# The second product of an MLP by Strassen's scheme, inside a fused attention and MLP kernel

## The chip, the cores and the metric

The kernel runs on one core of one Trainium2 chip. Times are device microseconds of that core. The engines are named as in the profile: PE does matrix products (PEld is its loading of weights), DVE is the vector engine, ACT the scalar engine with its function tables, POOL the general engine (here it masks, and issues the loads that convert f32 to f16), SP only issues DMAs. Every engine works off its own queue in order. Products are written to PSUM, eight banks of 512 f32 numbers per partition.

## The reference

Attention with a forgetting gate, for 8 batches, 8 heads, 576 tokens, head dimension 64, and then an MLP over all 4608 tokens:

```python
scores = q @ k.T / sqrt(64) + cum[i] - cum[j]      # cum: running sum of log f, causal mask
attn   = softmax(scores)
x      = (attn @ v)                                 # tokens x 512, heads side by side
h      = x @ w_in                                   # 512 -> 2048
g      = h - tanh(h)
out    = g @ w_out                                  # 2048 -> 512, f32
```

## The kernel before

**Attention pairs.** The heads of a batch are taken two at a time: 32 pairs p, pair p being heads 2c and 2c+1 of batch b, with p = 4b + c. For each pair `scores` (L256) makes seven tiles ti = 0 to 6 of transposed scores in PSUM; ACT takes the exponential (L262), POOL masks the diagonal blocks (L270). One pair later, between tiles 2 and 3, `values` (L280) multiplies by v, with a column of ones for the sums, and DVE divides (L284 to L286) into the tile xn.

**From attention to the MLP.** `turn` transposes xn into XR, a ring of 4 batches that holds x with the feature on the partition: for batch 0 by PE, from then on by two DMA transposes on SP's queue (L300: tokens 0 to 511 of the batch, L302: the last 64). It is emitted after tile 3 of the pair behind, so a batch's last pair (c = 3) is turned in the first pair of the next batch.

**The MLP** goes by units of 512 tokens, nine in all. A unit was a list of 32 steps: 16 `mlp1` steps, one for each block of 128 of the 2048 inner columns, and 16 `mlp2` steps. An `mlp1` step is four products of 128 x 128 x 512 (one for each c, in order) into one PSUM bank, tanh on ACT (L315), and an addition on DVE (L318) that leaves g for these 128 columns as an f16 tile gt. An `mlp2` step is four products of 128 x 128 x 512 (L326); four steps accumulate 128 tokens over all 16 blocks into one bank, ACT copies it to SBUF (L330), and SP stores it (L332).

**How they are mixed.** The MLP's steps are dealt out over the pairs. From pair 4 on, each pair takes the next `take` steps of the list of all units, and they are placed evenly between the pair's items (scores, values, transposes, turn), at the end of an item. The order on PE, POOL, SP and DVE is just the order of emission; each of these engines waits in that order. What is left of the list follows the last pair. `take` was 2 in pair 4, 8 in pair 5, 7 in pairs 6 to 9, then 8.

**Transposes of q and k.** For batches 0 to 2 PE transposes q and k (`trans`, L225) through PSUM, and DVE or ACT copies them out (L234); this goes on until pair 10. For later batches they are loaded by blocks (L86), turned by DMA into TQ and TK (L91, on SP's queue in the first two pairs of the batch before) and placed by DVE (L94).

**PSUM.** Two banks for scores, two for values, three (`ps_m`) that the MLP's tiles share in turn with the transposes of pairs 0 to 4, and one (`ps_tr`) for the later transposes. A buffer is given again when what reads it is done; for `mlp1` that is the addition on DVE.

**Loads.** w_in and w_out come in pieces of 1 MB (w_out is issued in pair 4); k, q and v of a batch come some pairs ahead, in pieces of 64 to 128 KB, issued by POOL after given tiles.

Of the kernel before, what the change touches and what calls it, by code (L numbers as in the profile page):

```python
# [8 lines left out]
FP32 = mybir.dt.float32  # L9
FP16 = mybir.dt.float16  # L10
AF = mybir.ActivationFunctionType
# [10 lines left out]
def kernel(  # L22
# [11 lines left out]
    P = 128  # L34
# [9 lines left out]
    qscale = float(D) ** -0.5  # L44
    inv_qscale = float(D) ** 0.5
    NFT = DFF // P
    NCH = DM // P
    UW = 512
    NU = NT // UW
# [3 lines left out]
    wpl = ctx.enter_context(tc.tile_pool(name="wpl", bufs=1))  # L53
    aex = ctx.enter_context(tc.tile_pool(name="aex", bufs=10))
    fin = ctx.enter_context(tc.tile_pool(name="fin", bufs=3))
    gtp = ctx.enter_context(tc.tile_pool(name="gtp", bufs=NFT + 6))
    tmp = ctx.enter_context(tc.tile_pool(name="tmp", bufs=2))
    PSUM = bass.MemoryType.PSUM
    ps_sc = ctx.enter_context(tc.tile_pool(name="ps_sc", bufs=2, space=PSUM))
    ps_av = ctx.enter_context(tc.tile_pool(name="ps_av", bufs=1, space=PSUM))  # L60
    ps_tr = ctx.enter_context(tc.tile_pool(name="ps_tr", bufs=1, space=PSUM))
    ps_m = ctx.enter_context(tc.tile_pool(name="ps_m", bufs=3, space=PSUM))

    win = wpl.tile([P, NCH, DFF], FP16)
    wout = wpl.tile([P, NFT, DM], FP16)
    RING = 4 * S
    XR = wpl.tile([P, NCH, RING], FP16)

# [39 lines left out]
    lf = cst.tile([NH, S], FP32)  # L108
# [9 lines left out]
    ones16 = cst.tile([NH, S], FP16)  # L118
    nc.vector.memset(ones16, 1.0)
    minus16 = cst.tile([2 * H, S], FP16)  # L120
# [13 lines left out]
    cum = cst.tile([NH, S], FP32)  # L134
    nc.vector.tensor_tensor_scan(out=cum, data0=ones16, data1=lf, initial=0.0,
                                 op0=ALU.mult, op1=ALU.add)
    chi = cst.tile([NH, S], FP16)
# [53 lines left out]
             (4, 2): [lambda: load_wout(NFT // 2, NFT)]}  # L191
    for n in range(NJ - 1):
        LOADS.setdefault((3, n), []).append(lambda n=n: load_v_block(1, n, 2, H))
    LOADS.setdefault((NPAIR, 5), []).append(lambda: load_qk(qn, q, 2, 0, H))
    LOADS.setdefault((NPAIR, 6), []).append(lambda: load_qk(kn, k, 2, 0, H))
    for b in range(2, B):
# [17 lines left out]
    E, XN, GT, M2 = {}, {}, {}, {}  # L214

    def trans(b, c, src, dst, early, copies):
        pn, g3 = S // NT6, NT6 // 2
        if early:
            t32 = ps_m.tile([P, UW], FP32, tag="m", name="t32")
            t16 = t32.bitcast(FP16)[:, 0:2 * S // 2].rearrange("p (a g n) -> p a g n", a=2, g=g3)  # L220
        else:
            t16 = ps_tr.tile([P, 2, g3, pn], FP16, tag="tr", name="t16")
        for a in range(2):
            for g in range(g3):
                nc.tensor.transpose(out=t16[:, a, g, :],  # L225
                                    in_=src[b % 2][:, 2 * c + a, 2 * g:2 * g + 2, :],
                                    identity=id16[0:pn, 0:pn])
        for e, eng in enumerate(copies):
            to = dst[b % 2][0:D, 2 * c:2 * c + 2, e:S:2].rearrange("d a (p g) -> d a p g", g=g3)
            of = t16[e * D:(e + 1) * D, :, :, :].rearrange("d a g p -> d a p g")  # L230
            if eng == "A":
                nc.scalar.activation(out=to, in_=of, func=AF.Copy)
            else:
                nc.vector.tensor_copy(out=to, in_=of)  # L234
# [66 lines left out]
                                    in_=xn[:, 0:NJ - 1, :].rearrange("p n d -> p (n d)"))  # L301
        nc.sync.dma_start_transpose(out=XR[:, c, r0 + S - D:r0 + S], in_=xn[D:P, NJ - 1, :])  # L302

    def mlp1(u, ft):
        hps = ps_m.tile([P, UW], FP32, tag="m", name="hps")
        t0 = u * UW % RING
        parts = [(0, t0, min(UW, RING - t0))]
        if t0 + UW > RING:
            parts.append((RING - t0, 0, t0 + UW - RING))
        for o, t, n in parts:  # L310
            for ci in range(NCH):
                nc.tensor.matmul(out=hps[:, o:o + n], lhsT=win[:, ci, ft * P:(ft + 1) * P],  # L312
                                 rhs=XR[:, ci, t:t + n], start=(ci == 0), stop=(ci == NCH - 1))
        th = tmp.tile([P, UW], FP32, tag="th", name="th")
        nc.scalar.activation(out=th, in_=hps, func=AF.Tanh, scale=-1.0)  # L315
        gt = gtp.tile([P, UW], FP16, tag="gt", name="gt")
        GT[(u, ft)] = gt
        nc.vector.tensor_tensor(out=gt, in0=hps, in1=th, op=ALU.add)  # L318

    def mlp2(u, s):  # L320
        m, part = divmod(s, 4)
        if part == 0:
            M2[u] = ps_m.tile([P, DM], FP32, tag="m", name="ops")
        ops = M2[u]
        for ft in range(part * 4, part * 4 + 4):
            nc.tensor.matmul(out=ops, lhsT=GT[(u, ft)][:, m * P:(m + 1) * P], rhs=wout[:, ft, :],  # L326
                             start=(ft == 0), stop=(ft == NFT - 1))
        if part == 3:
            ost = tmp.tile([P, DM], FP32, tag="ost", name="ost")
            nc.scalar.activation(out=ost, in_=ops, func=AF.Copy)  # L330
            r0 = u * UW + m * P
            nc.sync.dma_start(out=out[r0:r0 + P, :], in_=ost)  # L332

    pairs = [(b, c) for b in range(B) for c in range(NPAIR)]

    def att_items(p):
        def put(fn, *args):
            items.append((lambda: fn(*args), True))

        items = []  # L340
        here = pairs[p] if p < len(pairs) else None
        before = pairs[p - 1] if 0 < p <= len(pairs) else None
        after = pairs[p + 1] if p + 1 < len(pairs) else None
        early = p < NPAIR
        if p == 0:
            put(trans, *here, qn, QT, True, "AA")
            put(trans, *here, kn, KT, True, "VV")
        for ti in range(len(TILES)):
            if here:
                put(scores, *here, ti)  # L350
            for load in LOADS.get((p, ti), ()):
                items.append((load, False))
            if ti == 0 and after and after[0] < FAR:
                put(trans, *after, qn, QT, early, "VV")
            if ti == (1 if early else 3) and after and after[0] < FAR:
                put(trans, *after, kn, KT, early, "VV")
# [12 lines left out]
    at = 0  # L369
    with tc.manual_schedule(engines={PE, mybir.EngineType.Pool, mybir.EngineType.SP, mybir.EngineType.DVE}):  # L370
        for p in range(len(pairs) + 1):
# [47 lines left out]
```

## Time and profile before

Three runs took 361.14, 360.65 and 362.85 us. The profiled execution has a span of 363.2 us from its first instruction to its last; the page gives no other time for it.

| | us | of the span |
|---|---|---|
| PE busy | 345.8 | 95% |
| ACT busy | 219.5 | 60% |
| DVE busy | 196.4 | 54% |
| POOL busy | 162.8 | 45% |
| `mlp2` products (L326), 576 | 138.2 | |
| `mlp1` products (L312), 640 | 140.4 | |
| additions for gt (L318), 144 | 98.5 | |
| evictions of the output (L330), 36 | 21.5 | |
| copies of transposed q and k (L234) on DVE, 46 | 36.7 | |

Attention without MLP steps runs to about 40 us, attention with MLP steps to about 297, and then two units of MLP remain. A row of groups gives line, engine and operation, what is written and read with the shape, how often, and then the busy time and the mean of one in ns, and last the time that the engine stood idle just before and who ended it. A row of the chain of waits is a piece of the sequence that ended last: start, duration, what. In rows in order of time, brackets hold the idle time before and its releaser.

### The profile page before, as it was taken

The numbers are of one execution on the slowest core, as the hardware profiler recorded it, in microseconds if no ns is written. First come the engines' busy times: TensorE is split into PE (matmuls) and PEld (weight loads), VectorE is DVE, ScalarE is ACT, GpSimd is POOL, SyncE is SP. The second block draws the span as 40 slices with busy tenths as digits, with TensorE's granted clock in tenths as the row PEclk, the third lists the DMA queues.
The fourth block names the chain that finished last, engine by engine and source line by source line (L and its number), as shares of the span: only waits on it lengthen the run. The fifth ranks groups of instructions, "written<-read, shape, count | busy, mean of one in ns | idle before, by whom it ended". The sixth has DMA issues, their size and how long they took to land.

```text
span 363.2 us, 7383 instructions
## 1 busy us (share of the span) xinstructions
PE 345.8 (95%) x2724; PEld 190.8 (53%) x2724; DVE 196.4 (54%) x348; ACT 219.5 (60%) x415; POOL 162.8 (45%) x340
## 2 busy tenths in 40 slices
PE   1799999999999999999999999999999999999995
PEld 0466555555555555555557865555555544444442
DVE  7586699447981478147814682377227513712810
ACT  6567776457755785578657865686568634614721
POOL 7977663676176726763666367632222210000000
PEclk9999999999999999999999999999999999999999
DMA  9999999999999999999899989991220022011011
GB/s 106 152 196 189 155 202 119 127 139 150 97 63 137 156 147 73 138 156 147 60 144 171 130 68 136 167 143 25 76 74 18 18 81 67 3 58 58 2 44 72
DMA packets 140711, 38.72 MB, mean 107 GB/s; under 512 B 128084, under 2 KB 134980, under 8 KB 140676
## 3 DMA queue, kind: packets, MB, share of 16 engines
q0 software_dynamic: 92416, 18.37, 65.5%
q1 hardware_dynamic: 48260, 19.90, 27.5%
q8 instruction: 21, 0.34, 0.4%
q14 instruction: 14, 0.11, 0.1%
HBM read 36.85 MB, written 9.44 MB: 127 GB/s over the span
## 4 chain that ended last, share of the span: by engine, by line
PE 84%; DMA 4%; SPq 3%; DVE 3%; ACT 2%; issue 2%; POOL 1%; POOLq 0%; ACTq 0%
PE ops L326 31%; PE hps L312 31%; PE ps L256 12%; PE av L280 8%; DMA XR<-xn 2%; SPq L91 2%; PE t L225 2%; DMA TK<-kn 2%; ACT e L262 1%; DVE xn L286 1%; DVE KT L234 1%; DMA QT<-cq 1%; SPq L302 1%; PE x L297 1%; DVE gt L318 1%
## 5 line engine op out<-in xcount | busy, mean ns | idle before, releaser
L318 DVE TENSOR_TENSOR gt<-hps,th 128x512 f16<-128x512 f32 x144 | 98.5, 689 | 95.3 <-ACT th L315 94.6
L312 PE MATMUL hps<-XR,win 128*128 128x512 f16 (+1 forms) x640 | 140.4, 357 | 1.0 <-DMA XR<-xn 0.7
L326 PE MATMUL ops<-wout,gt 128*128 128x512 f16 x576 | 138.2, 379 | 0.0
L262 ACT ACTIVATE e<-ps 128x512 f16<-128x512 f32 x192 | 110.7, 598 | 26.1 <-PE ps L256 25.5
L315 ACT ACTIVATE th<-hps 128x512 f32<-128x512 f32 x144 | 86.7, 602 | 34.2 <-PE hps L312 31.3
L270 POOL TENSOR_SCALAR_AFFINE_SELECT e<-e 128x128 f16<-128x128 f16 (+1 forms) x192 | 64.8, 340 | 89.9 <-ACT e L262 87.1
L256 PE MATMUL ps<-QT,KT 67*128 67x64 f16 (+4 forms) x384 | 80.6, 295 | 6.0 <-DMA QT<-cq 4.2
L312 PEld LDWEIGHTS <-win 128*128 128x128 f16 x640 | 58.0, 97 | 50.1 <-issue 1.3
L326 PEld LDWEIGHTS <-gt 128*128 128x128 f16 x576 | 52.2, 97 | 54.2
L256 PEld LDWEIGHTS <-KT 67*128 67x128 f16 x384 | 37.7, 103 | 44.9 <-issue 6.6
L330 ACT ACTIVATE ost<-ops 128x512 f32<-128x512 f32 x36 | 21.5, 597 | 50.8 <-PE ops L326 49.0
L280 PEld LDWEIGHTS <-e 128*128 128x128 f16 x896 | 35.4, 102 | 7.4 <-POOL e L270 1.4
L280 PE MATMUL av<-vn,e 128*128 128x65 f16 x896 | 36.4, 199 | 0.6 <-POOL e L270 0.6
L105 POOL DMA_DIRECT2D vn<-in_v_dram x32 | 27.9, 875 | 2.6 <-issue 1.9
L286 DVE TENSOR_TENSOR xn<-av,rs 128x640 f16<-128x640 f32 x32 | 26.4, 825 | 1.1
L234 DVE COPY QT<-t 64x576 f16<-64x576 f16 x22 | 17.6, 802 | 14.7 <-PE t L225 14.6
L284 DVE TENSOR_SCALAR rs<-av 128x10 f32<-128x10 f32 x32 | 5.2, 161 | 35.4 <-PE av L280 34.0
L262 ACT ACTIVATE el<-ps 128x128 f16<-128x128 f32 x32 | 8.8, 274 | 25.3 <-PE ps L256 25.3
L270 POOL TENSOR_SCALAR_AFFINE_SELECT el<-el 128x128 f16<-128x128 f16 x32 | 9.4, 295 | 29.5 <-ACT el L262 29.1
L86 POOL DMA_DIRECT2D qn<-in_q_dram x25 | 21.4, 858 | 2.7 <-issue 2.7
L86 POOL DMA_DIRECT2D kn<-in_k_dram x25 | 21.2, 847 | 2.3 <-issue 2.3
L234 DVE COPY KT<-t 64x576 f16<-64x576 f16 x24 | 19.1, 796 | 0.2
(44 smaller groups left out, 111.1 us busy)
## 6 DMA issues: line engine op xcount, KB each, us to landing
out_dram<-ost SPq DMA_DIRECT2D x36, 256.0 KB
vn<-in_v_dram POOLq DMA_DIRECT2D x24, 128.0 KB, 5.6
qn<-in_q_dram POOLq DMA_DIRECT2D x20, 128.0 KB, 3.7
kn<-in_k_dram POOLq DMA_DIRECT2D x20, 128.0 KB, 5.6
win<-in_moe_w_in_dram POOLq DMA_DIRECT2D x2, 1024.0 KB, 10.6
wout<-in_moe_w_out_dram POOLq DMA_DIRECT2D x2, 1024.0 KB, 11.9
XR<-xn SPq DMA_TRANSPOSE x56
vn<-in_v_dram POOLq DMA_DIRECT2D x12, 64.0 KB, 5.4
```

The source lines that it names most:

```text
L86: nc.gpsimd.dma_start(out=dst[b % 2][0:pn, n, :].rearrange("p (h d) -> p h d", h=H), in_=src[b, :, n * P:n * P + pn, :].rearrange("h p d - ...
L105: nc.gpsimd.dma_start(out=vn[b % 2][:, n, h0:h1, 0:D], in_=v[b, h0:h1, n * P:(n + 1) * P, :].rearrange("h p d -> p h d"))
L234: nc.vector.tensor_copy(out=to, in_=of)
L256: nc.tensor.matmul(out=ps[:, col:col + n], lhsT=KT[b % 2][:, h, j * P:(j + 1) * P], rhs=QT[b % 2][:, h, i0:i0 + n])
L262: nc.scalar.activation(out=e[:, lo:hi], in_=ps[:, lo:hi], func=AF.Exp, scale=qscale)
L270: nc.gpsimd.affine_select(out=view, in_=view, compare_op=ALU.is_ge, fill=0.0, base=0, pattern=pat, channel_multiplier=-1)
L280: nc.tensor.matmul(out=av[:, a, ib, :], lhsT=E.pop((b, c, a, j, ib)), rhs=vn[b % 2][:, j, 2 * c + a, 0:D + 1], start=(j == 0), stop=(j == ib))
L286: nc.vector.tensor_tensor(out=xn.rearrange("p i (a d) -> p a i d", a=2), in0=av[:, :, :, 0:D], in1=rs.to_broadcast([P, 2, NJ, D]), op=ALU. ...
L312: nc.tensor.matmul(out=hps[:, o:o + n], lhsT=win[:, ci, ft * P:(ft + 1) * P], rhs=XR[:, ci, t:t + n], start=(ci == 0), stop=(ci == NCH - 1))
L315: nc.scalar.activation(out=th, in_=hps, func=AF.Tanh, scale=-1.0)
L318: nc.vector.tensor_tensor(out=gt, in0=hps, in1=th, op=ALU.add)
L326: nc.tensor.matmul(out=ops, lhsT=GT[(u, ft)][:, m * P:(m + 1) * P], rhs=wout[:, ft, :], start=(ft == 0), stop=(ft == NFT - 1))
```

## The change

The second product is done by the Winograd form of Strassen's scheme, once per unit. Of g (512 tokens x 2048) and w_out (2048 x 512), each is cut into four blocks: A11 and A12 are the first 256 tokens with the first and the second 1024 inner columns, A21 and A22 the other 256 tokens; B11 to B22 the blocks of w_out, 1024 x 256. Seven block products take the place of eight:

| step | product | where it goes |
|---|---|---|
| A11 B11 | m1 | copied out by ACT |
| S2 W2 | | u2 = m1 + it |
| A12 B21 | | out block (0,0) = m1 + it |
| S3 (B22-B12) | | u3 = u2 + it |
| S1 W1 | | out block (1,1) = u3 + it; u2 = u2 + it |
| A22 W4 | | out block (1,0) = u3 + it |
| S4 B22 | | out block (0,1) = u2 + it |

with S1 = A21 + A22, S2 = S1 - A11, S3 = A11 - A21, S4 = A12 - S2, and W1 = B12 - B11, W2 = B22 - W1, W4 = B21 - W2. The sums of blocks of A are f16, on DVE; those of w_out are formed once, in pair 6, eight operations of 128 x 1024; B12 is overwritten by B22 - B12.

A unit is now 16 + 14 = 30 steps. The `mlp1` steps alternate between the two halves of the inner columns; after every fourth step (a quad), DVE forms that quad's S1, S2 and S3. An `mlp2` step is eight products of 128 x 128 x 256; two steps make a block product of 256 tokens in one bank, which a DVE sum with an SBUF tile empties (ACT for the first). S4 is formed in place of A12 when A12 B21 is done. `take` becomes 2, 8, 7, 7, 6 in pairs 4 to 8 and then 8 and 7 in turn, and the transposes use the same PSUM buffers as the MLP, of which there are now four. To make room in SBUF, four tiles that are used at the start (log f, its running sum, ones, minus ones) are laid into TQ and TK.

```diff
-    gtp = ctx.enter_context(tc.tile_pool(name="gtp", bufs=NFT + 6))
+    gtp = ctx.enter_context(tc.tile_pool(name="gtp", bufs=5))
+    acc = ctx.enter_context(tc.tile_pool(name="acc", bufs=1))
...
-    ps_tr = ctx.enter_context(tc.tile_pool(name="ps_tr", bufs=1, space=PSUM))
-    ps_m = ctx.enter_context(tc.tile_pool(name="ps_m", bufs=3, space=PSUM))
+    ps_m = ctx.enter_context(tc.tile_pool(name="ps_m", bufs=4, space=PSUM))
...
+    for n in range(2):
+        ks = slice(n * NK // 2, (n + 1) * NK // 2)
+        for i, (o, x, y) in enumerate(((W1, B12, B11), (B12, B22, B12), (W2, B22, W1), (W4, B21, W2))):
+            LOADS.setdefault((NPAIR + 2, i), []).append(lambda o=o, x=x, y=y, ks=ks: nc.vector.tensor_tensor(
+                out=o[:, ks, :], in0=x[:, ks, :], in1=y[:, ks, :], op=ALU.subtract))
...
-    def mlp1(u, ft):
+    def mlp1(u, s):
+        pr, half = divmod(s, 2)
+        ft = half * NK + pr
...
-        gt = gtp.tile([P, UW], FP16, tag="gt", name="gt")
-        GT[(u, ft)] = gt
-        nc.vector.tensor_tensor(out=gt, in0=hps, in1=th, op=ALU.add)
+        if s % 4 == 0:
+            GQ[(u, s // 4)] = gtp.tile([P, 2, 2, UW], FP16, tag="gq", name="gq")
+        gq = GQ[(u, s // 4)]
+        nc.vector.tensor_tensor(out=gq[:, half, pr % 2, :], in0=hps, in1=th, op=ALU.add)
+        if s % 4 == 3:
+            sq = SQ[(u, s // 4)] = gtp.tile([P, 2, 2, HU], FP16, tag="sq", name="sq", bufs=4)
+            a11, a21 = gq[:, 0, :, 0:HU], gq[:, 0, :, HU:UW]
+            a22 = gq[:, 1, :, HU:UW]
+            for o, x, y, op in ((sq[:, 0], a21, a22, ALU.add), (sq[:, 1], sq[:, 0], a11, ALU.subtract),
+                                (a21, a11, a21, ALU.subtract)):
+                nc.vector.tensor_tensor(out=o, in0=x, in1=y, op=op)
...
+    STEPS = [("A11", B11), ("S2", W2), ("A12", B21), ("S3", B12), ("S1", W1), ("A22", W4), ("S4", B22)]
 
     def mlp2(u, s):
-        m, part = divmod(s, 4)
-        if part == 0:
-            M2[u] = ps_m.tile([P, DM], FP32, tag="m", name="ops")
-        ops = M2[u]
-        for ft in range(part * 4, part * 4 + 4):
-            nc.tensor.matmul(out=ops, lhsT=GT[(u, ft)][:, m * P:(m + 1) * P], rhs=wout[:, ft, :],
-                             start=(ft == 0), stop=(ft == NFT - 1))
-        if part == 3:
-            ost = tmp.tile([P, DM], FP32, tag="ost", name="ost")
-            nc.scalar.activation(out=ost, in_=ops, func=AF.Copy)
-            r0 = u * UW + m * P
-            nc.sync.dma_start(out=out[r0:r0 + P, :], in_=ost)
+        n, m = divmod(s, 2)
+        lhs, rhs = STEPS[n]
+        if m == 0:
+            M2["ps"] = ps_m.tile([P, 2, HE], FP32, tag="m", name="ops")
+        ps = M2["ps"]
+        for kt in range(NK):
+            nc.tensor.matmul(out=ps[:, m, :], lhsT=LHS[lhs](u, kt // 2)[:, kt % 2, m * P:(m + 1) * P],
+                             rhs=rhs[:, kt, :], start=(kt == 0), stop=(kt == NK - 1))
+        if m == 0:
+            return
+
+        def plus(src, to):
+            nc.vector.tensor_tensor(out=to, in0=ps, in1=src, op=ALU.add)
+            return to
+
+        def total(src, r, e):
+            ost = plus(src, tmp.tile([P, 2, HE], FP32, tag="ost", name="ost"))
+            r0 = u * UW + r * HU
+            nc.sync.dma_start(out=out[r0:r0 + HU, e * HE:(e + 1) * HE].rearrange("(m p) e -> p m e", p=P), in_=ost)
+
+        if lhs == "A11":
+            M2["m1"] = acc.tile([P, 2, HE], FP32, tag="m1", name="m1")
+            nc.scalar.activation(out=M2["m1"], in_=ps, func=AF.Copy)
...
+        elif lhs == "A12":
+            total(M2["m1"], 0, 0)
+            for i in range(4):
+                nc.vector.tensor_tensor(out=LHS["S4"](u, i), in0=LHS["A12"](u, i), in1=LHS["S2"](u, i), op=ALU.subtract)
...
-    mlp = [(fn, u, s) for u in range(NU) for fn in (mlp1, mlp2) for s in range(NFT)]
+    mlp = [(fn, u, s) for u in range(NU) for fn, n in ((mlp1, NFT), (mlp2, 2 * len(STEPS))) for s in range(n)]
+    TAKE = (0, 0, 0, 0, 2, 8, 7, 7, 6)
...
-            take = 0 if p < NPAIR else 2 if p == NPAIR else 7 if NPAIR + 1 < p <= 2 * NPAIR + 1 else 8
+            take = TAKE[p] if p < len(TAKE) else 8 - (p - len(TAKE)) % 2
```

More of the change, by code (lines that the diff above doesn't have):

```diff
@@ L46 @@
     NFT = DFF // P
+    NK = NFT // 2
+    HU = 256
+    HE = DM // 2
     NCH = DM // P
@@ L60 @@
     ps_av = ctx.enter_context(tc.tile_pool(name="ps_av", bufs=1, space=PSUM))
-    ps_tr = ctx.enter_context(tc.tile_pool(name="ps_tr", bufs=1, space=PSUM))
-    ps_m = ctx.enter_context(tc.tile_pool(name="ps_m", bufs=3, space=PSUM))
+    ps_m = ctx.enter_context(tc.tile_pool(name="ps_m", bufs=4, space=PSUM))
     win = wpl.tile([P, NCH, DFF], FP16)
     wout = wpl.tile([P, NFT, DM], FP16)
+    W1 = wpl.tile([P, NK, HE], FP16)
+    W2 = wpl.tile([P, NK, HE], FP16)
+    W4 = wpl.tile([P, NK, HE], FP16)
+    B11, B12 = wout[:, 0:NK, 0:HE], wout[:, 0:NK, HE:DM]
+    B21, B22 = wout[:, NK:NFT, 0:HE], wout[:, NK:NFT, HE:DM]
     RING = 4 * S
@@ L106, in load_v_block @@
                             in_=v[b, h0:h1, n * P:(n + 1) * P, :].rearrange("h p d -> p h d"))
-    lf = cst.tile([NH, S], FP32)
+    lf = TQ[0:NH, :, :].rearrange("p c s -> p (c s)").bitcast(FP32)[:, 0:S]
     nc.sync.dma_start(out=lf, in_=f.rearrange("b h s -> (b h) s"))
@@ L117 @@
     load_qk(kn, k, 0, 2, 4)
-    ones16 = cst.tile([NH, S], FP16)
+    ones16 = TK[0:NH, 0, :]
     nc.vector.memset(ones16, 1.0)
-    minus16 = cst.tile([2 * H, S], FP16)
+    minus16 = TK[0:2 * H, 1, :]
     nc.vector.memset(minus16, -1.0)
@@ L133 @@
         nc.vector.memset(KT[i][:, :, S:PITCH], 0.0)
-    cum = cst.tile([NH, S], FP32)
+    cum = TQ[0:NH, :, :].rearrange("p c s -> p (c s)").bitcast(FP32)[:, S:2 * S]
     nc.vector.tensor_tensor_scan(out=cum, data0=ones16, data1=lf, initial=0.0,
@@ L212, with trans @@
                     LOADS.setdefault((p0 + 3, 2 * n + a), []).append(lambda b=b, dst=dst, src=src, a=a, c=c: place(dst, src, b, a, c))
-    E, XN, GT, M2 = {}, {}, {}, {}
-    def trans(b, c, src, dst, early, copies):
+    E, XN, GQ, SQ, M2 = {}, {}, {}, {}, {}
+    def trans(b, c, src, dst, copies):
         pn, g3 = S // NT6, NT6 // 2
[L218 to L222, printed above, removed]
+        t32 = ps_m.tile([P, UW], FP32, tag="m", name="t32")
+        t16 = t32.bitcast(FP16)[:, 0:2 * S // 2].rearrange("p (a g n) -> p a g n", a=2, g=g3)
         for a in range(2):
@@ new lines @@
+    LHS = {"A11": lambda u, i: GQ[(u, i)][:, 0, :, 0:HU], "A12": lambda u, i: GQ[(u, i)][:, 1, :, 0:HU],
+           "A22": lambda u, i: GQ[(u, i)][:, 1, :, HU:UW], "S3": lambda u, i: GQ[(u, i)][:, 0, :, HU:UW],
+           "S1": lambda u, i: SQ[(u, i)][:, 0], "S2": lambda u, i: SQ[(u, i)][:, 1]}
+    LHS["S4"] = LHS["A12"]
+    STEPS = [("A11", B11), ("S2", W2), ("A12", B21), ("S3", B12), ("S1", W1), ("A22", W4), ("S4", B22)]
+    def mlp2(u, s):
+        n, m = divmod(s, 2)
[18 more added lines that the diff above has]
+            nc.scalar.activation(out=M2["m1"], in_=ps, func=AF.Copy)
+        elif lhs == "S2":
+            M2["u2"] = plus(M2["m1"], acc.tile([P, 2, HE], FP32, tag="u2", name="u2"))
+        elif lhs == "A12":
+            total(M2["m1"], 0, 0)
+            for i in range(4):
+                nc.vector.tensor_tensor(out=LHS["S4"](u, i), in0=LHS["A12"](u, i), in1=LHS["S2"](u, i), op=ALU.subtract)
+        elif lhs == "S3":
+            M2["u3"] = plus(M2["u2"], acc.tile([P, 2, HE], FP32, tag="u3", name="u3"))
+        elif lhs == "S1":
+            total(M2["u3"], 1, 1)
+            plus(M2["u2"], M2["u2"])
+        elif lhs == "A22":
+            total(M2["u3"], 1, 0)
+        else:
+            total(M2["u2"], 0, 1)
@@ L345, in att_items @@
         if p == 0:
-            put(trans, *here, qn, QT, True, "AA")
-            put(trans, *here, kn, KT, True, "VV")
+            put(trans, *here, qn, QT, "AA")
+            put(trans, *here, kn, KT, "VV")
         for ti in range(len(TILES)):
@@ L353, in att_items @@
             if ti == 0 and after and after[0] < FAR:
-                put(trans, *after, qn, QT, early, "VV")
+                put(trans, *after, qn, QT, "VV")
             if ti == (1 if early else 3) and after and after[0] < FAR:
-                put(trans, *after, kn, KT, early, "VV")
+                put(trans, *after, kn, KT, "VV")
             if ti == 2 and before:
```

## The prediction

> **What bounds the kernel now.** I read the page's busy table and slices first, then the groups with shapes kept apart, the chain of waits, and last the engines' rows in order of time around the places that the change touches.
>
> ```profile
> PE 345.8 (95%) x2724; PEld 190.8 (53%) x2724; DVE 196.4 (54%) x348; ACT 219.5 (60%) x415; POOL 162.8 (45%) x340
> PE   1799999999999999999999999999999999999995
> DVE  7586699447981478147814682377227513712810
> ```
>
> PE is full from the third slice on: what PE issues is the time. DVE looks half empty, but its slices swing between 1 and 9: it is the average of two kinds of stages. The stretches of the first MLP unit (512 tokens) and of the last show both:
>
> ```profile
> 45.60:62.30 16.70, 16.58 (x153) 9.09 (x152) 15.69 (x26) 12.74 (x25) 7.58 (x17) 1.00 1.61 172
> 303.96:317.77 13.81, 13.81 (x65) 6.26 (x64) 9.88 (x15) 9.57 (x16) 0.00 (x0) 1.00 0.06 21
> 317.77:331.58 13.81, 13.81 (x66) 6.24 (x64) 1.19 (x2) 2.39 (x4) 0.00 (x0) 1.00 0.15 57
> ```
>
> Busy us per engine in the order PE, PEld, DVE, ACT, POOL. While unit 0's first product runs beside attention with transposes (pairs 5 and 6), DVE works 15.69 of 16.70 us: it is nearly a second bound. In a second product it works 1.19 of 13.81.
>
> The chain of waits gives the pitch of the products, and one place that is nearly late:
>
> ```profile
> 196.74 1.75 PE hps L312 x16
> 224.94 7.01 DMA XR<-xn
> 317.77 13.81 PE ops L326 x64
> ```
>
> The sixteen in the first row are 256 columns wide (unit 4 wraps round the ring of XR), each with its own weights: 0.109 us. The last row's are 512 wide: 0.216 us. The middle row is the DMA transpose that brings a batch's last pair into XR. PE ran into its landing:
>
> ```profile
> 230.85 0.81 PE L312 MATMUL hps<-XR,win 128*128 128x512 f16 x3
> 232.00 0.38 PE L312 MATMUL hps<-XR,win 128*128 128x512 f16 x1 [0.34 <-DMA XR<-xn]
> ```
>
> Only the fourth product of a unit's first step needs that pair; it waited 0.34 us here and 0.32 at 81.54 (unit 1).
>
> **Part 1, the products.** Per unit 64 products of 0.2158 (13.81 us) become 7x2x8 = 112 of 0.1094 (12.25 us). Nine units: 14.0 us less on PE. PE is the bound, so this counts in full where nothing else comes late.
>
> **Part 2, what DVE gets.** These rows price it:
>
> ```profile
> L318 DVE TENSOR_TENSOR gt<-hps,th 128x512 f16<-128x512 f32 x144 | 98.5, 689 | 95.3 <-ACT th L315 94.6
> L286 DVE TENSOR_TENSOR xn<-av,rs 128x640 f16<-128x640 f32 x32 | 26.4, 825 | 1.1
> L94 DVE COPY KT<-TK 64x1152 f16<-64x1152 f16 x20 | 9.4, 509 | 0.3
> ```
>
> The seven sums of products with an SBUF tile have gt's form: 0.69, and in a run 0.60 (two gt in a row take 1.29). The f16 sums of two SBUF tiles have no row. gt and xn give 0.145 us plus 1.06 ns an element. An f16 copy that nothing disturbs took 0.44 to 0.46 us: 0.145 plus 0.27 ns an element. So 512 elements cost between 0.28 and 0.69, 1024 between 0.42 and 1.23. I take the pace that both rows share, counted by input bytes: gt reads 8 bytes an element, the copy 2, both some 7.6 bytes a ns. Two f16 inputs are 4 bytes: 0.42 us for 512 and 0.69 for 1024, in a run 0.33 and 0.60.
>
> Four steps of the first product (a quad) then add 1.2 us: the fourth gt and the first sum are each waited for by the next operation (0.10 and 0.03 over a run, as between rs and xn), then 0.42, 0.33, 0.33. Per unit: four quads 4.8, four sums for S4 1.3, seven sums of products 4.3, together 10.4; the weights 8 x 0.60 = 4.8 once. DVE rises by 98 us to 295. From pair 12 on a unit has four attention pairs, 37 us in the trace with 19.5 of DVE, so 29.9 fit: there it costs nothing, PE hides it. In three places it doesn't.
>
> *Pairs 5 and 6.* DVE was free for 1.0 us in 16.7, 0.7 after the first quad. Its order there gets four quads (4.8) and all eight weight sums (4.8), in a queue that it works strictly in turn: before gt of step 15 stand all weight sums and three quads. That gt ended at 61.74 and now ends 8.4 - 0.7 = 7.7 later, at 69.4. PE reaches the product that reads it (the eighth of A11) at 59.75 + 0.77 = 60.5. PE loses 8.9 us; behind the waiting product are pair 7's scores and transposes. With the ends for the f16 sums it is 5.5 or 16.
>
> *Pairs 9 and 10* (unit 1, transposes still on DVE: 3.2 us a pair, the rest of attention 1.2): pair 9 with 8 steps and 2 quads is 8x0.62 + 2.4 + 4.4 = 11.8 us of DVE against 9.6 of PE, pair 10 with 7 steps and 1 quad 9.9 against 8.7. The wait of Part 3 shortens PE's side of neither. Of the excess of 3.4 the four PSUM buffers and the wait for step 15 let some 1.9 pass: 1.5 us.
>
> *The two units after attention:* the first product has 16x0.62 + 4.8 = 14.7 of DVE to 13.8 of PE; PE may run three buffers ahead. I take 0.3 each, 0.6.
>
> **Part 3, where a unit begins.** A unit has 30 steps, not 32, and the list of steps per pair now puts each unit's first step right behind the first score of the pair after a batch's last. In the old order units 2 to 6 began two steps and two scores later. Between the end of that batch's last values products (V) and the fourth product of the new unit PE had 7.4 + 0.65 = 8.1 us; now it has four steps of 0.875, scores for 0.94, and 0.65: 5.1 us (unit 1: three steps and a transpose, 4.5). The transpose's landing records in the trace lie after V by 6.76, 7.68, 6.80, 7.36, 8.35 and 3.83 us for units 1 to 6. So PE waits 2.3, 2.6, 1.7, 2.6, 3.3 and 0 (unit 4's fourth narrow product comes 0.3 sooner): 12.5, less the 0.66 that it waits already: **11.8 us**. Nothing hides it: PE works in order, and behind the waiting product stand the pair's scores. The landings are long because loads of k and v are in the DMA queues (unit 6 has none: issue to landing 2.5 instead of 4.8 to 7.0). The loads keep their places in the pair. Before xn DVE now has two sums of S1 (xn 0.35 later), while k's loads start some 0.8 later after V since the pair is shorter: I let these cancel. Bounds: landings as short as unit 6's, no wait; 0.5 later each, 14.
>
> **Part 4, at nothing.** ACT loses 27 evictions (16 us) but no chain waited for ACT here. SP issues the same 36 stores of 256 KB, with one of them, as before, just ahead of the turn. POOL's queue is unchanged. Transposes take two of the four shared buffers per pair until pair 10; their release is by the DVE copies already counted (gain or loss within 1 us). The constants in TQ and TK are read long before pair 8 writes there. The last store comes behind 0.69 on DVE where 0.60 on ACT stood.
>
> **Sum:** -14.0 + 8.9 + 1.5 + 0.6 + 11.8 = +8.8 us on the profiled span of 363.2, so 372.0 there. The span lies 2.1 above the runs' median of 361.14; I add the same to that: **370**. About 1% is what a measurement of this kernel can tell from no change.
>
> **Rivals.**
> - *The forecast*, both waits: 364 to 378, 47%.
> - *Both covers hold*, faster: DVE's extra work goes into PE's lead, and XR lands in time because a pace with fewer stores ahead empties the DMA queues, as in unit 6's row. Then only 14.0 and the 0.66 go: 346 to 352. It decides if landings stay under 5.1 us after V and the f16 sums run at the copy's pace. Against it: five of six landings are above 6.7. 8%.
> - *XR in time, DVE late:* -14.7 + 11.0 = 357.5 (355 to 361). 13%.
> - *XR late, DVE hidden* (the weights finish in the lead): -14.0 + 11.8 + 0.6 = 359.5. Against it: 15.69 of 16.70. 10%.
> - *The f16 sums run at gt's pace:* pairs 5 and 6 cost 16, each quad 2.0 not 1.2, which makes unit 1 lose 4 and the last two units 4 each: -14 + 16 + 4 + 8 + 11.8 = +26, 387 (380 to 396). 12%. The trace's one f16 SBUF row is far from gt's pace, which speaks against it; copies that ran beside POOL's work took up to 0.86 us, which speaks for something like it. [...]
> - *PE's clock falls in the waits.* In the trace 30 values products took 1.65 us until 38 us and 0.91 after, so there is a half speed; afterwards PE never paused over 0.62 us, and now it would, for 1.7 to 3.3 us five times. If each costs 2 to 3 us at half speed, +10 more: 380. [...] 7%.
> - *The change doesn't do what it says:* 256-wide products with weights from sums stall on weight loads (97 ns each, hidden in the row above): at 0.12 us the gain is 3 us, 381. 3%.
>
> Range: 8% below and about 10% above left out: **355 to 384**. Faster 17% (both covers; half of the third; a little of the fourth), same 18%, slower 65%.
>
> **What would show it.** Products at L353 in runs of 16 taking 1.75 us; the f16 sums near 0.42; PE idle for some 9 us in pairs 5 and 6 with DVE as releaser and DVE full; PE idle before hps five times, released by the XR transpose, 1.7 to 3.3 us each; slices after 310 us full. The forecast is wrong if XR lands within 5 us of the values, or if PE's lead covers the weights.

## The result, and the profile after

The changed kernel takes 392.4 us (the middle one of 391.87, 392.38 and 395.56) where the kernel before takes 361.14: 1.085 times as long, with a 95% interval of 1.077 to 1.094. A fourth run of each kernel, of 398.01 us after and of 1864.21 before, was a slow one, over 1.5% above the fastest of its kernel, and is not counted. The forecast was 370, in a range of 355 to 384. It had the sign and most of the places, and little more than a quarter of the size. The profiled execution of the changed kernel took 392.38 us, with a span of 390.7 (before 363.2).

The page of the changed kernel, busy times and slices, and below it the clock's slices of the kernel before:

```profile
PE 344.6 (88%) x3156; PEld 235.0 (60%) x3156; DVE 295.9 (76%) x563; ACT 206.9 (53%) x388; POOL 166.9 (43%) x340
...
PE   1898977988989799969998899969999999999995
...
DVE  7678998775999378936886588728896866876973
...
PEclk9999995998999899998999899969999999999999
```

```profile
PEclk9999999999999999999999999999999999999999
```

DVE's total of 295.9 is the forecast 295. What is new is in the two PE rows: PE is no longer full, and its granted clock, which before stood at 9 throughout, has a dip at the start of each of units 1 to 5 and a deep one at slice 7, in pairs 5 and 6. (The page's slices are 9.8 us here; the clock was 0.999 on average before and is 0.960 now. The clock's records begin with the first grant of full clock; ahead of it the row shows 9 too, though the 30 values products of a pair take 1.65 us there and 0.91 after it.)

The groups with shapes kept apart give the prices that no row had before: the f16 sums of four-step quads (L338: S1, S2, S3), of S4 (L375) and of the weights (L205).

```profile
L331 DVE TENSOR_TENSOR gq<-hps,th 128x512 f16<-128x512 f32 x144 | 96.1, 687 | 44.7 <-ACT th L327 42.2
L338 DVE TENSOR_TENSOR gq<-gq 128x512 f16<-128x512 f16 x36 | 16.9, 471 | 0.0
L338 DVE TENSOR_TENSOR sq<-gq 128x512 f16<-128x512 f16 x36 | 15.6, 433 | 1.2
...
L375 DVE TENSOR_TENSOR gq<-gq,sq 128x512 f16<-128x512 f16 x36 | 14.1, 452 | 0.0
L205 DVE TENSOR_TENSOR W<-wout,W 128x1024 f16<-128x1024 f16 x4 | 2.7, 705 | 0.0
```

The forecast estimated 0.42 and 0.69 for these: they take 0.43 to 0.47 and 0.68 to 0.71. The products are as forecast too. Two pieces of the chain of waits of the changed kernel, one beside attention and one in the tail (start, duration, what):

```profile
283.45 1.75 PE ops L353 x16
...
347.25 11.64 PE ops L353 x105
```

Sixteen narrow products with their sixteen weights take 1.75 us, 0.109 each (0.111 in the tail); per unit 112 of them are 12.25 us, and nine units save the 14.0 us.

The waits, summed by who waits for whom (total, times, longest):

```profile
PE hps L324 <- DMA XR<-xn: 16.6, 5, 4.1
DVE ost L359 <- DMA out_dram<-ost: 12.5, 6, 3.4
PE hps L324 <- DVE gq L331: 5.0, 8, 2.0
PE ops L353 <- DVE gq L331: 3.7, 6, 1.9
```

The first row is the forecast wait for the DMA transpose at the start of units 1 to 5, the last two are DVE being late, and the second (DVE waiting until an output tile has been stored) is not in the forecast at all. One of the five, at unit 2, in PE's rows (the bracket is the idle time before):

```profile
133.87 0.38 PE L324 MATMUL hps<-XR,win 128*128 128x512 f16 x1 [2.49 <-DMA XR<-xn]
...
134.30 1.85 PE L324 MATMUL hps<-XR,win 128*128 128x512 f16 x4
```

After the wait of 2.49 us four products take 1.85 us, and the next four 1.72, instead of some 0.87: PE runs on, but at half its pace. The trace's clock records (they are what the PEclk row is made of) say the same. They hold half clock from 134.35 for 3.41 us, and also from 59.26 for 10.24, from 89.98, 175.31 and 216.27 for 3.41 each, and from 257.23 for 6.83: 30.7 us together, all of it behind pauses of PE (what follows the last product is left out). In the kernel before no pause between 40 us and the end was over 0.63 us, and the clock never fell.

**Where the time came from.** The profiled execution of before reached full clock at 38.0 us, that of after at 25.1; this makes the values products issued in pair 5 start at 45.6 and at 41.4, 4.2 us apart, before the change can have any say. So I count from there to the end of the last product: 313.6 us before, 345.0 after, +31.4. (31.4, less 4.2, plus 0.2 at the very end, is the 27.4 between the spans of 390.67 and 363.23.)

| | forecast | measured |
|---|---|---|
| products | -14.0 | -14.0 |
| PE idle in pairs 5 and 6 | +8.9 | +6.2 |
| PE idle, pairs 9 and 10 | +1.5 | +2.1 |
| PE idle, waits for XR (16.6 less the 0.66 of before) | +11.8 | +15.9 |
| PE idle in later pairs, other | 0 | +1.9 |
| PE idle, last two units | +0.6 | +2.0 |
| half clock: 30.7 us less 2.7 idle in it, by a half | 0 | +14.0 |
| sum | +8.8 | +28.1 |

Of the 3.3 that are left to 31.4, 1.0 lies in the last two units: three pauses of each count 0.98 us by the idle times of the rows, and 1.46 by the starts of the products around them. Another 0.6 is work of PE in pairs 5 and 6 (19.59 us there at full clock, in a run below, against 19.01 before). Where the other 1.7 lies is not shown.

### The profile page after: what moved, and what is told of

Same layout as the page of the kernel before. It is cut to its first block, busy times and chain, and to the rows that moved or that the text cites. A ratio compares the mean times of both kernels' runs of the same rounds, so it can differ in the third digit from the quotient of the medians.

```text
span 390.7 us, 8437 instructions
## 1 busy us (share of the span) xinstructions
PE 344.6 (88%) x3156; PEld 235.0 (60%) x3156; DVE 295.9 (76%) x563; ACT 206.9 (53%) x388; POOL 166.9 (43%) x340
## 5 line engine op out<-in xcount | busy, mean ns | idle before, releaser
L324 PE MATMUL hps<-XR,win 128*128 128x512 f16 (+1 forms) x640 | 150.7, 373 | 21.7 <-DMA XR<-xn 16.6
L331 DVE TENSOR_TENSOR gq<-hps,th 128x512 f16<-128x512 f32 x144 | 96.1, 687 | 44.7 <-ACT th L327 42.2
L280 POOL TENSOR_SCALAR_AFFINE_SELECT e<-e 128x128 f16<-128x128 f16 (+1 forms) x192 | 68.3, 360 | 111.6 <-ACT e L272 109.1
L324 PEld LDWEIGHTS <-win 128*128 128x128 f16 x640 | 60.7, 101 | 60.7 <-issue 14.1
L266 PE MATMUL ps<-QT,KT 67*128 67x64 f16 (+4 forms) x384 | 81.6, 295 | 9.2 <-DMA KT<-clo 3.3
L353 PEld LDWEIGHTS <-gq 128*128 128x128 f16 x720 | 68.3, 98 | 18.2 <-DVE gq L331 4.3
L353 PE MATMUL ops<-wout,gq 128*128 128x256 f16 x576 | 75.1, 276 | 3.8 <-DVE gq L331 3.7
L353 PE MATMUL ops<-W,sq 128*128 128x256 f16 x288 | 36.1, 273 | 0.0
L359 DVE TENSOR_TENSOR ost<-ops,u 128x512 f32<-128x512 f32 x27 | 18.6, 690 | 22.1 <-DMA out_dram<-ost 12.5
L353 PEld LDWEIGHTS <-sq 128*128 128x128 f16 x288 | 26.9, 98 | 3.8
L296 DVE TENSOR_TENSOR xn<-av,rs 128x640 f16<-128x640 f32 x32 | 26.4, 825 | 1.1
L244 DVE COPY QT<-t 64x576 f16<-64x576 f16 x22 | 17.6, 802 | 7.5 <-PE t L235 7.4
L272 ACT ACTIVATE el<-ps 128x128 f16<-128x128 f32 x32 | 8.8, 275 | 24.3 <-PE ps L266 24.2
```

What stands on the lines that cost most here:

```text
L266: nc.tensor.matmul(out=ps[:, col:col + n], lhsT=KT[b % 2][:, h, j * P:(j + 1) * P], rhs=QT[b % 2][:, h, i0:i0 + n])
L272: nc.scalar.activation(out=e[:, lo:hi], in_=ps[:, lo:hi], func=AF.Exp, scale=qscale)
L280: nc.gpsimd.affine_select(out=view, in_=view, compare_op=ALU.is_ge, fill=0.0, base=0, pattern=pat, channel_multiplier=-1)
L296: nc.vector.tensor_tensor(out=xn.rearrange("p i (a d) -> p a i d", a=2), in0=av[:, :, :, 0:D], in1=rs.to_broadcast([P, 2, NJ, D]), op=ALU. ...
L331: nc.vector.tensor_tensor(out=gq[:, half, pr % 2, :], in0=hps, in1=th, op=ALU.add)
L353: nc.tensor.matmul(out=ps[:, m, :], lhsT=LHS[lhs](u, kt // 2)[:, kt % 2, m * P:(m + 1) * P], rhs=rhs[:, kt, :], start=(kt == 0), stop=(kt ...
```

## The experiments

Theory: two things make the loss. First, DVE has been given work in a stretch in which it was full (pairs 5 and 6); second, the new list of steps puts a unit's first step where XR hasn't landed. To both, the clock that falls in the pauses adds about as much as the pauses themselves. Rivals: the loss is DVE's throughout; or the clock is a mere symptom; or the shared PSUM banks, not the sums, cost the early pairs. The kernels of one group ran beside a run of the kernel before on their chip (359.96 for the first four, 362.85 for the next four). Single runs are compared from the values of pair 5 on, since full clock came at different times: at 38.0 us in the trace of before, at 25.1 in that of after.

### Two steps later

```diff
-    TAKE = (0, 0, 0, 0, 2, 8, 7, 7, 6)
+    TAKE = (0, 0, 0, 0, 2, 8, 7, 7, 4)
```

> One number differs from the changed kernel: pair 8 takes 4 steps, not 6, so that units 1 to 6 begin two steps later in their pair, as in the kernel before. Theory: most of the loss comes from PE's waits for the XR transpose at the start of units 1 to 5 (16.6 us in the changed kernel's trace) and from the stretches at half clock right behind them (four of 3.4 us, one of 6.8). Two steps and two scores give 2.2 us more room; the landings lay 7.7 to 9.3 us after the values, the room becomes 7.3: waits of 0.4 to 2.0 us each, some 5 in all, and the clock should stay whole at most of them. 11 us of waits and 8 us of half clock go: span 372 instead of 390.7. Rival: DVE, busy 76% of the span, is the bound, and the waits only take its place: the span stays above 385. Second rival: the waits go but the clock still falls: 379.

375.7 us, with a span of 374.0. From pair 5 on it takes 324.1, which is 20.9 less than the change. PE's clock by slices, from its page, and a row of its waits:

```profile
PEclk9999999599999999999999999999999999999999
```

```profile
DVE ost L359 <- DMA out_dram<-ost: 17.7, 5, 5.0
```

Only one dip of the clock is left, that of pairs 5 and 6 (10.24 us from 65.4), and of the wait for XR 1.8 us. So the place of a unit's first step, with what the clock adds, costs two thirds of the loss, without one operation less on any engine. DVE now waits 17.7 us for stores.

### Four steps later

```diff
-    TAKE = (0, 0, 0, 0, 2, 8, 7, 7, 6)
+    TAKE = (0, 0, 0, 0, 2, 8, 7, 7, 2)
```

> As the run before, with 2 steps in pair 8: units 1 to 6 begin four steps later than in the changed kernel, some 4.3 us more room (9.4 after the values). Theory: no wait for XR is left and the clock stays whole from 70 us on: 16.6 and 9 us go, span 365, with the loss in pairs 5 and 6 (PE idle 6 us, half clock for 10 us) still in it. If DVE is the bound: above 385.

A plain miss: 423.0 us. Expected was the last of the XR waits gone and nothing else. SP's queue and DVE's rows at one unit's start show what else there is:

```profile
275.83 7.18 SPq L99 DMA_TRANSPOSE TQ<-qn  x5
283.11 4.54 SPq L365 DMA_DIRECT2D out_dram<-ost  x3
```

```profile
286.57 0.69 DVE L359 TENSOR_TENSOR ost<-ops,u 128x512 f32<-128x512 f32 x1 [6.46 <-DMA out_dram<-ost]
```

SP issues five DMA transposes of q for 7.18 us, and a unit's stores stand behind them in the same queue. There are two output tiles, so the third sum into one waits for the first one's store, here 6.46 us. Before the change it was ACT that filled these tiles, and no product waited for it; now it is DVE, and behind the waiting sum stand the additions that empty PSUM for PE. In the changed kernel the same waits (12.5 us) end before XR lands, and no wait of PE is put down to them.

### Full PE in the wait

```diff
+        if s == 0 and 1 <= u <= 5:
+            for i in range(16):
+                nc.tensor.matmul(out=hps, lhsT=win[:, 0, ft * P:(ft + 1) * P], rhs=win[:, 1, 0:UW], start=True, stop=True)
```

Sixteen products more per unit, in front of the first step of units 1 to 5; their result is overwritten.

> The changed kernel with 16 more products of 512 columns (3.45 us) whose results are overwritten, ahead of the first step of units 1 to 5, where PE otherwise waits for XR. Theory on the clock: PE's waits there (2.5 to 4.1 us) are filled, the same time passes, but PE isn't idle, so the five stretches at half clock (20 us, costing some 9) don't come: span 382. If the half clock comes from something else than PE's idleness there (the loads, the DVE's load), the stretches stay and the span is 391; if the waits were not what PE does there (the products add), 391 + 17 = 408.

384.7 us: 80 products more, and faster than the change. From pair 5 on 338.2, 6.8 less. The waits for XR are gone from the list of waits but for 0.2 us (the time passes in the added products), and of the clock's dips there remain pairs 5 and 6, and a new one of 3.41 us at 111.4 has come, as the clock's slices on its page show:

```profile
PEclk9999996899989999999999999999999999999998
```

The added work does nothing but keep PE busy, so this is the clock's own price: 20.5 us at half clock are gone and 3.4 new, which by a half is 8.5; 6.8 were gained. A fallen clock is no mere symptom.

### No sums of weights

```diff
-    for n in range(2):
-        ks = slice(n * NK // 2, (n + 1) * NK // 2)
-        for i, (o, x, y) in enumerate(((W1, B12, B11), (B12, B22, B12), (W2, B22, W1), (W4, B21, W2))):
...
-    STEPS = [("A11", B11), ("S2", W2), ("A12", B21), ("S3", B12), ("S1", W1), ("A22", W4), ("S4", B22)]
+    STEPS = [("A11", B11), ("S2", B22), ("A12", B21), ("S3", B12), ("S1", B12), ("A22", B21), ("S4", B22)]
```

The eight sums of w_out's blocks are left out, and the products read blocks of w_out in their place, so the output is not the MLP's.

> The changed kernel without the eight sums of w_out's blocks in pair 6; the products S2, S1 and A22 read blocks of w_out instead, so the output is that of another scheme, at the same cost on PE. Theory: pairs 5 and 6 lose some 11 us because DVE's queue has 4.8 us of quads and 5.2 us of weight sums more than before, and because the clock then stands at half from 59 to 69 us. Without the weight sums PE's longest idle stretches there (2.0 and 1.9 us) go: DVE 5.2 us less, and 1 to 4 us of half clock: span 382 to 385. Rival: the quads alone keep DVE full there: a gain below 2 us.

386.9 us. Pairs 5 and 6 by engine (start:end, length, then PE, PEld, DVE, ACT, POOL with their instructions, PE's clock, DMA share, GB/s); first this kernel, then the changed one, then the one before:

```profile
40.86:64.21 23.35, 19.59 (x186) 12.04 (x185) 22.29 (x40) 14.24 (x28) 9.30 (x20) 1.00 1.16 147
```

```profile
41.40:71.43 30.03, 23.67 (x186) 13.67 (x185) 27.06 (x48) 14.40 (x28) 10.13 (x20) 0.83 0.96 117
```

```profile
45.59:64.72 19.13, 19.01 (x171) 10.43 (x170) 17.33 (x28) 13.58 (x27) 8.86 (x20) 1.00 1.43 152
```

In the changed kernel DVE has 48 instructions there where it had 28, and they fill it; PE's 23.67 busy us for the same 186 instructions that take 19.59 without the sums are the clock (0.83 on average). Eight operations of 4.8 us on DVE thus cost 6.7 us of time: the clock stays up without them. The waits for XR stay (17.6 us, five times), with their dips of the clock (0.968 on average over the span); from pair 5 on it is 340.0. The two stretches are separate losses.

### Four steps later, with four output tiles

```diff
-            ost = plus(src, tmp.tile([P, 2, HE], FP32, tag="ost", name="ost"))
+            ost = plus(src, tmp.tile([P, 2, HE], FP32, tag="ost", name="ost", bufs=4))
...
-            M2["u3"] = plus(M2["u2"], acc.tile([P, 2, HE], FP32, tag="u3", name="u3"))
+            M2["u3"] = plus(M2["u2"], acc.tile([P, 2, HE], FP32, tag="m1", name="u3"))
...
-    TAKE = (0, 0, 0, 0, 2, 8, 7, 7, 6)
+    TAKE = (0, 0, 0, 0, 2, 8, 7, 7, 2)
```

> The run with 2 steps in pair 8 (units begin four steps later), and the output's staging tile ost in four buffers, not two (u3 shares m1's buffer to make room). Theory: that run lost so much because two stores of a unit fell behind the five TQ transposes in SP's queue (6.5 to 7.5 us), the third sum of the unit waited for a buffer of ost, and behind it in DVE's queue stood all that PE needs: DVE waited 25.8 us for stores, PE's units began 3 to 5.5 us late, and the clock fell at each. With four buffers no sum waits for a store: DVE's waits for stores below 2 us, no wait of PE over 2 us after 70 us, span 365 to 372 instead of 420. Rival: the later begin itself is bad (XR or DVE's load), and the store was only the name on the wait: span above 400.

391.6 us: half right. From pair 5 on 31.3 of the 375.5 us of the run with two tiles are gone, and with them every wait of DVE for a store, so these made 31 us of that miss. But the time is far from 365 to 372: PE's second product waits 21.9 us for additions, in five long pauses above all, in A11 B11. PE's and DVE's rows at unit 4 (brackets: idle before):

```profile
239.98 0.28 PE L353 MATMUL ops<-wout,gq 128*128 128x256 f16 x1 [3.37 <-DVE gq L331]
```

```profile
236.36 0.69 DVE L331 TENSOR_TENSOR gq<-hps,th 128x512 f16<-128x512 f32 x1
236.97 1.18 DVE L102 COPY KT<-TK 64x1152 f16<-64x1152 f16 x2
...
238.50 0.82 DVE L296 TENSOR_TENSOR xn<-av,rs 128x640 f16<-128x640 f32 x1
239.24 1.28 DVE L331 TENSOR_TENSOR gq<-hps,th 128x512 f16<-128x512 f32 x2
```

Four steps later, a unit's last quad falls into the end of a batch, where DVE places q and k (L102) and divides the values (L294 to L296): 2.4 us of it stand between one addition of the quad and the next ones, which the product waits for. Behind four of the five pauses, of 3.4 to 3.5 us each, the clock falls (0.963 on average over the span): behind the one above, eight products take 1.90 us from 241.55 on, where the eight at 240.32 took 1.04. A shift along the list takes a unit away from one late thing and into the next.

### Two steps later, with four output tiles

The same edit, with `TAKE` 4 in pair 8.

> Four buffers of ost with 4 steps in pair 8 (units begin two steps later; without the buffers 374.0, with 17.7 us of DVE waits for stores and PE waits of 0.5 to 0.9 us at the units' beginnings). Theory: DVE's waits for stores go, and with them some 0.7 us of PE waits a unit: span 368 to 371; the trace's pairs 5 to 7 still lose 11 us. The first 45 us vary by 4.5 us from run to run with the time at which the clock becomes whole, so it is compared from pair 5's values on: 324.1 before, 319 to 321 expected. Rival: no change, the sums' waits lay in DVE's free time.

369.6 us; from pair 5 on 322.0, 2.1 less than without the tiles, where 3 to 5 less were expected (319 to 321). What is left beside the kernel before (313.6) lies in pairs 5 to 11: 68.9 us from the values of pair 5 to those of pair 11, where it took 56.9. From there to the end this kernel is 3.6 us *faster* than before (253.1 against 256.7).

### The sums of weights on POOL

```diff
-            LOADS.setdefault((NPAIR + 2, i), []).append(lambda o=o, x=x, y=y, ks=ks: nc.vector.tensor_tensor(
+            LOADS.setdefault((NPAIR + 2, i), []).append(lambda o=o, x=x, y=y, ks=ks: nc.gpsimd.tensor_tensor(
```

> As the run with four buffers and units two steps later, and the eight weight sums on POOL, not DVE. Theory: they stand in DVE's queue ahead of what PE waits for, and without them (left out altogether) pairs 5 to 7 took 6.7 us less. On POOL they cost 1.1 to 2.2 us each, some 9 to 18 us beside masks and loads in pair 6: the masks come later, but PE reads them a pair later. If DVE's queue is what counts, 4 to 6 us less than the run beside it; if POOL's delay of the masks or the shared access of DVE and POOL to SBUF takes its place, no gain or a loss.

366.6 us, 3.0 less (2.8 from pair 5 on); 4 to 6 were expected. DVE's and POOL's rows say where the rest went:

```profile
55.72 2.34 DVE L338 TENSOR_TENSOR gq<-gq 128x512 f16<-128x512 f16 x1
```

```profile
55.47 4.57 POOL L205 TENSOR_TENSOR wout<-wout 128x1024 f16<-128x1024 f16 x2
```

A sum takes POOL 2.3 us where it took DVE 0.7, and a sum of two SBUF tiles on DVE that begins beside one took 2.34 us instead of 0.42. In pairs 5 and 6 the four S3 sums cost 1.38 each on the mean; the additions that read PSUM (L331) stay at 0.68.

### And one copy in four on ACT

```diff
-                put(trans, *after, qn, QT, "VV")
+                put(trans, *after, qn, QT, "AV")
```

> As the run with the weight sums on POOL, and of the four copies per pair of transposed q and k one goes from DVE to ACT (0.80 us each on both). If DVE is still the bound in pairs 5, 6, 9 and 10, it gains 0.8 us in each of these, 3 us in all; ACT's share there, 12.7 of 16.7 us before, has room for 0.8 a pair. If ACT is then late with tanh or exponentials: no gain.

366.9 us; from pair 5 on 318.9 against 319.2, so 0.3 us gained where 3 were expected. Part of the reason stands in the rows: PE's long pause in pair 6 is still there (2.14 us, before 2.18), and in pairs 8 and 9 the next copy on DVE waits for the one on ACT, for 1.16 and 1.74 us, where it had waited 0.32 and 0.90 for PE. The clock had one dip more, of 3.41 us at 25.7 (0.984 on average, 0.990 without the copy), but ahead of pair 5. The rest is not settled.

### The first unit by the old scheme

If pairs 5 to 10 have no room on DVE, the scheme need not be used there. Unit 0 is done as in the kernel before; the weights' sums move to pairs 7 and 9, where unit 0's second product leaves DVE idle; there are four output tiles, and the later units begin two steps later, as above, because unit 0 has its 32 steps again.

```diff
-        if s % 4 == 3:
+        if s % 4 == 3 and u > 0:
...
-    mlp = [(fn, u, s) for u in range(NU) for fn, n in ((mlp1, NFT), (mlp2, 2 * len(STEPS))) for s in range(n)]
+    mlp = [(fn, u, s) for u in range(NU) for fn, n in ((mlp1, NFT), (mlp2, 2 * len(STEPS)) if u else (plain, NFT)) for s in range(n)]
```

> Unit 0 is done as in the kernel before (32 steps, eight products of 512 columns by four steps, evicted by ACT); units 1 to 8 by the new scheme, with four buffers for the output and the unit starts two steps later; the weights' sums stand on DVE in pairs 7 and 9, where unit 0's second product leaves it room. My theory: what is lost in pairs 5 to 10 is lost to DVE's sums in a stretch where DVE was full already. Then values of pair 5 to values of pair 11 is back at 57 to 59 us (before 56.9, with the sums on POOL 66.9), the later pairs keep the 3.3 us and the tail the 1.0 us that they gained with the sums on POOL, and the time is 357 to 360 where the kernel before takes 361. Rival: the stretch is lost because transposes and MLP share four PSUM banks, or because of the alternating order of the inner columns; both are unchanged here, and the time stays at 365 to 368.

358.74 us (357.43 to 360.21, ten runs) against 361.39 of the kernel before on that chip (thirteen runs): 0.992 times, 0.989 to 0.995, a gain of under 1%. Pairs 5 and 6 in the same view as above:

```profile
41.00:60.12 19.12, 18.90 (x171) 10.43 (x170) 18.10 (x30) 13.58 (x27) 9.31 (x20) 1.00 1.58 182
```

19.12 us, as before the change (19.13), with the shared PSUM banks and the alternating order of the inner columns still in place: the rival that blamed these for the loss in pairs 5 and 6 falls. From the values of pair 5 to those of pair 11 it takes 59.2.

### And A12 B21 second

In the runs whose units begin two steps later one small wait is left in each of units 1 to 4: between A11's products and S2's, PE waits 0.63 to 0.70 us for the last quad's f16 sums. A12 B21 does not need them.

```diff
-    STEPS = [("A11", B11), ("S2", W2), ("A12", B21), ("S3", B12), ("S1", W1), ("A22", W4), ("S4", B22)]
+    STEPS = [("A11", B11), ("A12", B21), ("S2", W2), ("S3", B12), ("S1", W1), ("A22", W4), ("S4", B22)]
```

> As the run before it, and the second and third block product change places: A11 B11, A12 B21, S2 W2, ... . In all earlier runs PE waits once per unit between A11's products and S2's for the last quad's f16 sums (0.66 us beside attention, 0.5 in the tail), which A12 B21 does not need. If that wait is only latency, 1.75 us of products in between hide it: 0.6 us less in each of units 1 to 6 and 0.5 in units 7 and 8, together 4 to 5 us, 353 to 355. If DVE is late by more than that, or the sums for S4 come late instead, the time stays within 1 us of the run before.

355.70 us (355.61 to 360.38, four runs): 0.987 times the kernel before, 0.980 to 0.994. It is 3.0 us less than the run before it (2.9 from pair 5 on), where 4 to 5 were expected: the expectation counted the wait in eight units, but the trace of the run before has it in four, 2.7 us in all. PE's rows at unit 4, first in the old order, then in the new:

```profile
214.03 0.39 PE L370 MATMUL ops<-W,sq 128*128 128x256 f16 x2 [0.65 <-DVE sq L339]
```

```profile
213.94 1.91 PE L370 MATMUL ops<-wout,gq 128*128 128x256 f16 x16
```

Beside attention the wait is gone. In the last two units PE still pauses for 0.50: there A12 B21 itself waits for the addition of step 15, because DVE is behind by then. This kernel's page has a 9 in every slice of the clock, and the longest pause of PE after 40 us is 0.97 us. From pair 5 on it takes 308.8 us, 4.8 less than the kernel before (313.6), so most of the gain does not hang on when full clock came. So the scheme does pay here, by a little over 1%: 4.8 of the 12.5 us that eight units of it take off PE.

## Why the prediction was wrong

**Part 1, the products, was right**: 1.75 us for sixteen, 14.0 us in all. So were **the prices of the f16 sums** and DVE's total; the rivals that hung on these (sums at gt's pace, stalls on weights) fall.

**Pairs 5 and 6: the mechanism was right, and its size was nearly right by chance.** DVE is full and its order is the one forecast: the addition that the eighth product of A11 waits for ends 24.3 us after the start of pair 5's values, 23.8 by the forecast. But that product waits only 1.88 us; 4.2 of PE's pauses come ahead of it, in the first product, which waits for DVE's additions to free PSUM banks. PE idles 6.2 us where 8.9 were forecast, and the stretch became 10.9 us longer (30.03 against 19.13): the half clock, 10.24 us less 2.15 idle in it, adds 4.0, and PE's work itself is 0.6 more (19.59 without the sums, at full clock, against 19.01). Without the sums of weights 6.7 of it went away.

**The step that failed first is the clock.** The prediction had "PE's clock falls in the waits" as a rival, at 7%, with 2 to 3 us for each of five waits; it is not a rival but a term of the sum, which the forecast put at nothing: +14.0 by the records, and 6.8 gained with the added products at units 1 to 5 alone. Even the rival left it out in pairs 5 and 6, and no run shows its 2 to 3 us: half clock stood for 3.41 us behind each of four waits and for 6.83 behind the fifth. That PE would keep full clock through the waits was the author's estimate; the trace of before could not show it, with no pause over 0.63 us from 40 us on. In the changed kernel the six stretches of half clock begin whole multiples of 3.41 us apart (at 59.26, 89.98, 134.35, 175.31, 216.27 and 257.23), and in the 3.41 us just ahead of them PE paused for 2.35, 3.10, 2.49, 3.37, 2.80 and 3.41: only ahead of the last, at unit 5, was it idle throughout. The 2.49 at unit 2 (130.94 to 134.35) is one pause, the 2.35 in pairs 5 and 6 is pauses of 2.04 and 0.31. The longest pause at full clock that brought none there was 1.62 us. It is PE's scores of pair 10 that wait so long for a copy of k, in the changed kernel and in the run with the added products:

```profile
112.38 0.39 PE L266 MATMUL ps<-QT,KT 67*128 67x512 f16 x1 [1.62 <-DVE KT L244]
```

```profile
111.17 0.45 PE L266 MATMUL ps<-QT,KT 67*128 67x512 f16 x1 [1.62 <-DVE KT L244]
```

The first brought no dip; behind the second came the one at 111.4. Two pauses of the same length went two ways, and what decided it is not shown. (The ends of products are modelled in the trace, so a small difference between the two would not show.)

**Part 3, where a unit begins: right in place, 4.1 us short.** PE reached the product 4.7 to 5.4 us after the values, 4.6 to 5.2 by the forecast's own count (it starts at the modelled end of the values, 0.2 us after the start of the next product, from which I count), against 4.5 to 5.1 forecast. But XR landed 8.29, 7.69, 8.81, 8.12 and 9.26 us after the values for units 1 to 5, and by the same count 6.95, 7.85, 6.96, 7.53 and 8.54 in the kernel before: 1.3, 1.9, 0.6 and 0.7 us later for units 1, 3, 4 and 5, and 0.2 sooner for unit 2. The term that was mis-sized is "xn 0.35 later", and the choice to let it cancel against k's loads. DVE's rows at unit 3, where the values end at 166.41:

```profile
166.32 0.69 DVE L359 TENSOR_TENSOR ost<-ops,u 128x512 f32<-128x512 f32 x1
166.92 0.68 DVE L359 TENSOR_TENSOR u<-ops,u 128x512 f32<-128x512 f32 x1
167.52 0.16 DVE L294 TENSOR_SCALAR rs<-av 128x10 f32<-128x10 f32 x1
```

The division begins 1.1 us after the values, behind both sums of S1; before the change it began after 0.2. So xn ends 0.6 to 0.9 us later at units 2 to 5, and SP issues XR's transpose 0.9, 0.7 and 0.9 us later at units 3, 4 and 5: at units 4 and 5 that is the whole delay. At units 1 and 3 another 1.0 us lies between issue and landing; no run here takes it apart. Unit 6 had no wait, as forecast, and from its start to unit 7's first product it is 35.15 us, where before it was 35.60.

**Part 4, "at nothing", was wrong about the stores.** The sentence counted SP's stores, which are the same, and not who waits for them. Two output tiles were enough for ACT; for DVE they make 12.5 us of waits in the changed kernel (over before XR lands), 17.7 with the units two steps later (2.1 us of time), and 25.8 with four steps (31.3 us of time).

**The last two units:** 0.3 each was forecast, 1.46 each was lost, so that a unit takes 27.51 us where it took 27.62. A quad costs DVE 3.87 us (four additions 2.69, three sums 1.18) and PE 3.45, and ahead of the fourth quad PE begins to wait. DVE's and PE's rows:

```profile
341.23 2.69 DVE L331 TENSOR_TENSOR gq<-hps,th 128x512 f16<-128x512 f32 x4
343.96 0.42 DVE L338 TENSOR_TENSOR sq<-gq 128x512 f16<-128x512 f16 x1
...
```

```profile
341.96 3.61 PE L324 MATMUL hps<-XR,win 128*128 128x512 f16 x16 [0.23 <-DVE gq L331]
...
347.25 1.16 PE L353 MATMUL ops<-wout,gq 128*128 128x256 f16 x9 [0.49 <-DVE gq L331]
```

The forecast took 0.62 for an addition in a run; it is 0.67, which over sixteen is 0.8 us, about what three buffers of lead were to cover. In the tail, then, an eighth of the second product's work came off PE and nearly all of it was given back by DVE.

What stays open: 1.7 us between the table's sum and the measured difference, why XR's transposes of units 1 and 3 took 1.0 us longer from issue to landing and the others did not, and most of why a copy on ACT gains nothing.

## What to carry to other kernels

Cost a new wait of the engine that bounds a kernel twice, once as idle time and once at the clock that follows: here the pauses took some 28 us and the half clock behind them another 14. Work that goes from a full engine to a half-empty one must be placed against the second engine's load stage by stage, and where one stage has no room, leave that stage as it was: the scheme lost 8.5% as it was put in, and gained 1.3% with the first unit left alone, the units' starts where XR has landed, two more output tiles and two products exchanged. When a sum moves to another engine, ask what it waits for there (output tiles, a queue of stores) and what stands behind it.

## What the runs showed of the hardware that was not expected

- In the changed kernel PE's clock fell to a half in six stretches, of 3.41, 6.83 and 10.24 us, that begin whole multiples of 3.41 us apart; in the 3.41 us ahead of each, PE had paused for 2.35 to 3.41 us. A pause of 1.62 us brought none there, and one of 1.62 us did in the run with the added products.
- At the start, under the same attention work, full clock came at 38.0 us in the profiled execution of before and at 25.1 in that of after, and the values of pair 5 started 4.2 us apart. In the last experiment's four runs the profiled one, with full clock at 37.8, took 360.38 and the others 355.61 to 355.78; that these had it earlier is likely, but no trace of them is at hand.
- A DVE sum of two SBUF tiles that began beside POOL's sums of two SBUF tiles took 2.34 us where 0.42 was usual, and a sum on POOL took some three times as long as on DVE (2.1 to 2.3 against 0.7 us for 128 x 1024).
